# Padded value products, another loop order and two candidate lists in a local attention kernel with routed experts

## The chip, the cores and the metric

The kernel runs on one core of one Trainium2 chip. The metric is the time of one execution in device microseconds (us); less is better. Engines are named as in the profile: PE is TensorE's products, PEld its weight loads, DVE is VectorE, ACT ScalarE, POOL GpSimd, SP SyncE. An engine name with a q (SPq) is that engine's queue, which issues DMAs.

## What is computed

Attention inside blocks of 64 tokens, and then eight experts with one expert per token and at most `capacity` (80) tokens each. Shapes: q, k and v are 8 x 8 x 576 x 64 in float32; 4608 tokens with 512 features; experts of 512 x 1024 x 512.

```python
scores = scale * np.matmul(q_c, k_c.transpose(0, 1, 2, 4, 3))   # blocks of 64
attn = np.exp(scores - np.max(scores, axis=-1, keepdims=True))
attn = attn / (np.sum(attn, axis=-1, keepdims=True) + 1e-09)
x = np.matmul(attn, v_c)                     # then tokens x 512
logits = x @ w_gate
expert_idx = np.argmax(logits, axis=1)
gate_w = softmax(logits)[np.arange(N), expert_idx]
for e in range(E):
    tok_idx = np.where(expert_idx == e)[0]
    if len(tok_idx) > capacity:              # keep those of the highest gates
        gw = gate_w[tok_idx]
        tok_idx = tok_idx[np.argpartition(-gw, capacity)[:capacity]]
    h = np.maximum(x[tok_idx] @ w1[e], 0.0)
    out[tok_idx] = gate_w[tok_idx, None] * (h @ w2[e])
```

Tokens that no expert keeps stay zero in the output.

## The kernel before

Attention. The tokens go through in 18 blocks of 256 tokens, `j`; iteration `i` of the loop takes up several blocks at different stages. `scores(i)` multiplies q and k in tiles of 64 x 64, `maxima(i)` and `shift(i)` on VectorE take the row maximum off, `probs(j)` turns the result on TensorE (`turned`, into the PSUM tile `tp`) and ScalarE writes exp of it to `pT`. `values(j, c)` multiplies `pT` by v for half c of the block: per call 16 products of 64 rows, 64 columns of output and 65 columns of v (the 65th is ones, so that the row sum comes along), each of them two instructions in float32, into the PSUM tile `o`, of which there is one. `divide(j, c)` on VectorE divides by the row sum and `store(j, c)` writes x to HBM. `xtrans(j)` turns x on TensorE, through `tp` as well, and ScalarE copies it. After two blocks `gate_mm` and `gate_sum` (lines 408 to 425) give the logits of four tiles of 128 tokens.

Every engine takes its instructions in the order in which they are written. Small gating steps wait in two queues, `gates` and `bounds_q`, and `fill` (VectorE), `pe_slot` (TensorE) and `act_slot` (ScalarE) put some of them into the written order of the loop.

Routing. A token's key is its gate weight. `lev` compares the keys of four tiles with 256 levels per expert (signs on ScalarE, steps on VectorE) and `tally` counts on TensorE how many lie above each, and `threshold` finds the level above which an expert has at least its capacity; this waits for all 36 tiles, the last eight of them in the interleaved order `LAST`. The keys above it get a place in the list (a mask, a scan and three products, lines 855 to 873), `hot` writes one-hot matrices and 36 products gather one list of at most 128 candidates per expert, `cand`. `rank` compares each candidate with all 128 on VectorE, `select` makes one-hot columns, and `place` puts them into 6 groups of 128 slots (four groups of 32 slots each; an expert has 96). `gi0` and `gi1` are the token rows that are to be gathered, `si` (line 949) those to which the results are written.

Experts. For each group r of 128 slots: gather x rows by an indirect DMA, turn them, layer one, turn, layer two, scatter. The 32-slot quarters of a group belong to experts `groups[r]`: 0001, 1122, 2333, 4445, 5566, 6777. The weights of a layer (2 MB) come whole. Those of experts 0 and 1 are issued early, as eight pieces of 1 MB at the end of iteration 15 (`early_weights`, lines 669 to 677 and 785). Layer one of expert 2 is issued before the experts, layer one of expert 3 after `si` is known, and all the others by `ahead(r)` behind it on SyncE's queue in the order that it lists. `clear(n)` writes zeros to a ninth of the output: four before the experts, five within `ahead(1)`.

## Time and profile before

| what | value |
|---|---|
| median of 3 runs | 290.91 us (290.15 to 293.84) |
| the profiled execution: its time, its span | 290.53 us, 288.7 us |
| busy: PE, PEld, DVE, ACT, POOL | 228.4, 141.9, 118.3, 72.9, 31.0 us |
| instructions: PE and PEld, all | 4193 and 4193, 9408 |
| granted TensorE clock, mean | 0.858 |
| DMA | 85.0 MB, mean 294 GB/s; 418 GB/s from 240 to 260 us |
| instruction fetches (queue q8) | 35 packets, 0.57 MB |
| DMAs issued by SyncE | v 36 x 260 KB, q and k 35 x 512 KB, x 36 x 256 KB, weights 8 x 1024 KB and 12 x 2048 KB, zeros 9 x 1024 KB |

The span runs from the first to the last instruction; the execution's time has a little around it. A busy share is an average over stages with different limits, so the stages are read one by one: the loop, its end, the routing, the experts.

### The profile page before, as it was taken

To read this page: it belongs to the slowest core of one execution; us is meant where nothing else is said; L and a number is where in the kernel's file an instruction comes from. 1 tells how busy PE (TensorE), PEld (TensorE's weight loads), DVE (VectorE), ACT (ScalarE), POOL (GpSimd) and SP (SyncE) were. 2 spreads that over 40 slices of the span, in tenths; PEclk is the share of its full clock that TensorE was granted. 3 is DMA by queue.
4 is the path that set the end of the run, shared out by engine and by line. 5 is a ranking of instruction groups with operands and counts; after the bars stand their busy time and mean duration, and the time that the engine had idled before them with its cause. 6 is when DMAs were issued, how large, how long until landed. Compare 5 with 4: busy or idle time off the path is not lost.

```text
span 288.7 us, 9408 instructions
## 1 busy us (share of the span) xinstructions
PE 228.4 (79%) x4193; PEld 141.9 (49%) x4193; DVE 118.3 (41%) x333; ACT 72.9 (25%) x120; POOL 31.0 (11%) x81
## 2 busy tenths in 40 slices
PE   8466976897787799720644797989999999999990
PEld 6456764776476788620443475833333242423320
DVE  0746587378385578730363056621111111111110
ACT  1212433145444253630154232013001020201000
POOL 2200000002001001000120044260000011100011
PEclk9957799689597779985595559899999999999997
DMA  7999899969889869999749900179999999996011
GB/s 273 338 407 401 280 344 345 333 221 359 279 294 319 270 206 293 396 419 398 293 170 401 346 40 2 35 236 390 413 419 417 419 418 420 419 416 277 1 36 33
DMA packets 28624, 85.00 MB, mean 294 GB/s; under 512 B 3169, under 2 KB 3425, under 8 KB 28577
## 3 DMA queue, kind: packets, MB, share of 16 engines
q1 hardware_dynamic: 27328, 80.86, 74.7%
q0 software_dynamic: 960, 2.88, 2.9%
q8 instruction: 35, 0.57, 0.9%
q10 hardware_dynamic: 288, 0.59, 0.5%
q14 instruction: 13, 0.10, 0.1%
HBM read 64.14 MB, written 20.45 MB: 293 GB/s over the span
## 4 chain that ended last, share of the span: by engine, by line
PE 66%; DMA 10%; issue 9%; ACT 5%; DVE 5%; POOL 2%; POOLq 0%; ACTq 0%; SPq 0%; DVEq 0%
PE hc L193 15%; PE yc L226 14%; PE o L379 9%; PE s L337 7%; DMA v<-in_vv 6%; PE px L359 5%; PE pt L359 4%; PE lg L423 4%; ACT pT L367 4%; PE L L412 3%; DMA qk<-in_qk 2%; DMA ct<-in_cst 2%; PE hpc L211 2%; ACT lv L506 1%; PE pwarm L661 1%
## 5 line engine op out<-in xcount | busy, mean ns | idle before, releaser
L379 PE MATMUL o<-v,pT 64*64 64x65 f32 x1152 | 30.8, 250 | 23.8 <-DMA v<-in_vv 14.3
L193 PE MATMUL hc<-w,xtc 128*32 128x512 f32 x384 | 43.4, 594 | 0.2 <-ACT xtc L183 0.2
L226 PE MATMUL yc<-w,htc 128*32 128x512 f32 x384 | 42.3, 592 | 0.0
L379 PEld LDWEIGHTS o<-v,pT 64*64 64x64 f32 x1152 | 25.7, 159 | 27.1 <-DMA v<-in_vv 14.4
L367 ACT ACTIVATE pT<-pt 128x1024 f32<-128x1024 f32 x18 | 18.4, 1024 | 70.4 <-PE pt L359 70.4
L337 PE MATMUL s<-qk 64*64 64x64 f32 x1152 | 25.9, 249 | 5.9 <-DVE sm L349 2.7
L345 DVE TENSOR_REDUCE mx<-s 128x16 f32<-128x1024 f32 x18 | 22.0, 1222 | 14.1 <-PE s L337 14.0
L337 PEld LDWEIGHTS s<-qk 64*64 64x64 f32 x1152 | 24.0, 164 | 6.8 <-issue 6.5
L226 PEld LDWEIGHTS yc<-w,htc 128*32 128x32 f32 x384 | 12.4, 110 | 28.3 <-issue 28.3
L392 DVE TENSOR_TENSOR x<-o,rc 128x512 f32<-128x512 f32 x36 | 24.9, 691 | 0.8
L193 PEld LDWEIGHTS hc<-w,xtc 128*32 128x32 f32 x384 | 11.8, 110 | 26.0 <-issue 25.5
L405 ACT COPY xT<-px 128x1024 f32<-128x1024 f32 x18 | 18.2, 1012 | 20.6 <-PE px L359 20.5
L388 DVE TENSOR_SCALAR rc<-o 128x8 f32<-128x8 f32 x36 | 5.9, 163 | 42.6 <-PE o L379 42.6
L349 DVE TENSOR_TENSOR sm<-s,mx 128x1024 f32<-128x1024 f32 x18 | 21.8, 1213 | 0.1
L359 PE MATMUL px<-ct,x 64*128 64x64 f32 x288 | 16.3, 266 | 6.9 <-ACT pT L367 6.3
L359 PEld LDWEIGHTS px<-ct,x 64*128 64x128 f32 x288 | 13.2, 171 | 15.0 <-ACT pT L367 14.1
L198 ACT ACTIVATE hsc<-hc 128x512 f32<-128x512 f32 x6 | 3.6, 599 | 63.3 <-PE hc L193 57.9
L231 DVE TENSOR_SCALAR ysc<-yc,gatec 128x512 f32<-128x512 f32 x6 | 4.5, 752 | 33.4 <-PE yc L226 33.4
L359 PE MATMUL pt<-ct,sm 64*128 64x64 f32 x288 | 14.3, 244 | 1.1 <-issue 1.1
L232 POOL DMA_INDIRECT out<-ysc,si x6 | 6.0, 994 | 83.7 <-DMA out<-zero 41.1
L423 PEld LDWEIGHTS lg<-fold,lt 128*128 128x128 f32 x72 | 13.2, 279 | 2.8 <-ACT lt L417 2.4
L423 PE MATMUL lg<-fold,lt 128*128 128x8 f32 x72 | 13.9, 325 | 0.7 <-ACT lt L417 0.7
(135 smaller groups left out, 217.3 us busy)
## 6 DMA issues: line engine op xcount, KB each, us to landing
w<-in_w SPq DMA_DIRECT2D x12, 2048.0 KB, 22.1
qk<-in_qk SPq DMA_DIRECT2D x35, 512.0 KB, 5.9
v<-in_vv SPq DMA_DIRECT2D x36, 260.0 KB, 5.5
xs<-x SPq DMA_DIRECT2D x36, 256.0 KB, 4.1
out<-zero SPq DMA_DIRECT2D x9, 1024.0 KB, 18.0
w<-in_w SPq DMA_DIRECT2D x8, 1024.0 KB, 12.7
qk<-in_qk ACTq DMA_DIRECT2D x1, 512.0 KB, 5.0
ct<-in_cst SPq DMA_DIRECT2D x1, 326.0 KB, 7.4
```

What stands on the lines that cost most here:

```text
L193: nc.tensor.matmul(h[o:o + 32, :], lhsT=xT[r][:, b, o:o + 32], rhs=getw(groups[r][g])[0][:, b, 512 * f:512 * f + 512], start=(b == 0), sto ...
L226: nc.tensor.matmul(y[o:o + 32, :], lhsT=hT[r][c // 4][:, c % 4, o:o + 32], rhs=getw(groups[r][g])[1][:, c, :], start=(c == 0), stop=(c == ...
L337: nc.tensor.matmul(ps[64 * u:64 * u + 64, h, o:o + 64], lhsT=q[64 * h:64 * h + 64, pr, u, :], rhs=k[64 * h:64 * h + 64, pr, u, :], start=T ...
L345: nc.vector.tensor_reduce(mx, PR[j]['s'], axis=AX.X, op=ALU.max)
L349: nc.vector.tensor_tensor(sm.rearrange("p a h k -> p h a k"), PR[j]['s'], PR[j]['mx'][:, :, :, None].to_broadcast([P, 2, 8, 64]), op=ALU.s ...
L359: nc.tensor.transpose(pm[:, u, 64 * a:64 * a + 64], src(a)[rows], ident[rows, rows])
L367: nc.scalar.activation(pT, pm, AF.Exp, scale=0.125)
L379: nc.tensor.matmul(po[64 * u:64 * u + 64, h, 65 * pr:65 * pr + 65], lhsT=PR[j]['pT'][rows, u, a:a + 64], rhs=v[rows, pr, u, :], start=True ...
L392: nc.vector.tensor_tensor(PR[j]['x'][:, c, :].rearrange("p (m h e) -> p h m e", h=2, m=4), po[..., 0:64], rc[:, :, :, None].to_broadcast([ ...
L405: nc.scalar.copy(XT[T][:, j % 2].rearrange("p a u t -> p u a t"), pm.rearrange("p u (a t) -> p u a t", a=8))
L412: nc.tensor.matmul(pl[32 * pr:32 * pr + 32].rearrange("p (r t) -> p r t", r=4), lhsT=wgp[:, pr], rhs=xT[:, pr], start=True, stop=True, til ...
L423: nc.tensor.matmul(lg[:, 4 * n + r, :], lhsT=S['lt', T][:, r], rhs=fold, start=True, stop=True)
```

## The change

- v is laid into four standing tiles `vz` of 128 partitions x 2 x 520, zeroed once. The rows of one head go to the even partitions and to the first half of the columns, those of the other head to the odd partitions and the second half; the rest stays zero. `shift` writes its result with the two heads interleaved to match. A product then has 128 rows and 130 columns and does both heads: 8 products per call of `values` instead of 16. Each v load becomes two, one per head.
- The loop's order: before, `xtrans(i-3)`, `values(i-2, 0)`, `scores(i)`, `maxima`, `values(i-2, 1)`, `shift(i)`, `probs(i-1)`; now `scores(i)`, `maxima`, `xtrans`, `values(., 0)`, `shift`, `probs`, `values(., 1)`. The gate sums and level counts are spread over more iterations (`SUMS`).
- The eight early weight pieces are issued two per iteration from i = 15, the last two behind the stores of block 17. Two clears instead of four stand before the experts, seven within `ahead(1)`.
- The threshold comes from the first 32 tiles (28 to 31 counted on VectorE). Their candidates make a first list, those of tiles 32 to 35 above the same threshold a second one, of at most 128 each. Every rank is a comparison with both lists (256 columns, a constant in `lev_t` settling ties), once for each list, and every placing adds two products. The slots are placed in three parts: group 0, group 1, groups 2 to 5, each with its `targets`.

The core of the diff; `positions(r0, r1)` is the old mask, scan and three products for tiles r0 to r1, `gather_up` the old gathering loop, `listed` the key sum and copy.

```diff
+LATE = 32
...
-                IN['v', j, c] = wk.tile([P, 520], F32, name=f"v{j}_{c}", tag=f"v{c}", bufs=2)
-                nc.sync.dma_start(IN['v', j, c], vv[j, c])
+                for h in range(2):
+                    nc.sync.dma_start(vz[j % 2, c][h:P:2, h], vv[j, c, h])
...
-            sm = PR[j]['sm'] = wk.tile([P, 8, 2, 64], F32, name=f"sm{j}", tag="sm")
+            sm = PR[j]['sm'] = wk.tile([P, 8, 64, 2], F32, name=f"sm{j}", tag="sm")
             nc.vector.tensor_tensor(
-                sm.rearrange("p a h k -> p h a k"), PR[j]['s'],
+                sm.rearrange("p a k h -> p h a k"), PR[j]['s'],
...
-            v = IN['v', j, c].rearrange("p (a u x) -> p a u x", a=4, u=2)
+            v = vz[j % 2, c].rearrange("p h (a u x) -> p h a u x", a=4, u=2)
             for pr in range(4):
-                for h in range(2):
-                    for u in range(2):
-                        rows = slice(64 * h, 64 * h + 64)
-                        a = 64 * (4 * c + pr)
-                        nc.tensor.matmul(
-                            po[64 * u:64 * u + 64, h, 65 * pr:65 * pr + 65],
-                            lhsT=PR[j]['pT'][rows, u, a:a + 64],
-                            rhs=v[rows, pr, u, :], start=True, stop=True)
-            PR[j]['o', c] = po[:, :, 0:260].rearrange("p h (m x) -> p h m x", m=4)
+                o, a = 130 * (pr % 2), 64 * (4 * c + pr)
+                for u in range(2):
+                    nc.tensor.matmul(
+                        po[64 * u:64 * u + 64, pr // 2, o:o + 130].rearrange(
+                            "p (h x) -> p h x", h=2),
+                        lhsT=PR[j]['pT'][:, u, a:a + 64],
+                        rhs=v[:, :, pr, u, :], start=True, stop=True)
+            PR[j]['o', c] = po[:, :, 0:260].rearrange("p j (m x) -> p j m x", m=4)
...
-            nc.vector.scalar_tensor_tensor(ge, U[32]['ph'], 0.5, left, op0=ALU.mult, op1=ALU.is_ge)
+            nc.vector.scalar_tensor_tensor(ge, U[LATE - 4]['ph'], 0.5, left, op0=ALU.mult, op1=ALU.is_ge)
...
+            io_h = gk.tile([P, P, HOT], BF16, name="io_h", tag="io_h", bufs=1)
...
+            vz = {}
+            for b in range(2):
+                for c in range(2):
+                    vz[b, c] = wk.tile([P, 2, 520], F32, name=f"vz{b}{c}", tag=f"vz{b}{c}", bufs=1)
+                    nc.vector.memset(vz[b, c], 0.0)
...
+                p.tensor_copy(io_h, ct[:, C_IO + P:C_IO + 2 * P, None].to_broadcast([P, P, HOT]))
...
-            SUMS = {7: (0, 1), 9: (2,), 13: (3, 4), 15: (5,), 17: (6,)}
+            SUMS = {7: (0, 1), 9: (2,), 11: (3,), 13: (4,), 15: (5,), 17: (6,)}
             for i in range(NP_):
                 now[0] = i
                 if i == 2:
                     late_constants()
+                scores(i)
+                load_qk(i + 3, 0)
+                maxima(i)
+                fill(2)
                 if i >= 3:
                     xtrans(i - 3)
+                pe_slot()
                 if i >= 2:
                     values(i - 2, 0)
                     load_v(i, 0)
                     divide(i - 2, 0)
                     store(i - 2, 0)
-                scores(i)
-                load_qk(i + 3, 0)
-                pe_slot()
-                maxima(i)
-                fill(2)
+                    fill()
+                shift(i)
+                load_qk(i + 3, 1)
                 now[0] = i + 0.5
                 act_slot(2)
+                if i >= 1:
+                    probs(i - 1)
+                    if i == 1:
+                        warm_up(8)
+                fill(2)
                 if i >= 2:
                     values(i - 2, 1)
                     load_v(i, 1)
                     divide(i - 2, 1)
                     store(i - 2, 1)
                     fill()
-                load_qk(i + 3, 1)
-                shift(i)
-                fill(2)
-                if i >= 1:
-                    probs(i - 1)
-                    if i == 1:
-                        warm_up(8)
                 if i >= 4 and i % 2 == 0:
                     gate_mm((i - 4) // 2)
                 if i in SUMS:
...
-                    if i == 13:
-                        gates.append(("v", lambda: lev(12, 20, "av")))
-                    if i == 15:
-                        gates.append(("v", lambda: lev(20, 24, "a")))
-                    if i == 17:
-                        gates.append(("v", lambda: lev(24, 28, "v")))
+                    if i in (11, 13, 15, 17):
+                        gates.append(("v", lambda r=2 * i - 10: lev(r, r + 4, "a")))
                 pe_slot()
                 act_slot(3)
                 fill(2)
-                if i == 15:
-                    for n in range(8):
-                        early_weights(n)
+                if i >= 15:
+                    for n in range(2):
+                        early_weights(2 * (i - 15) + n)
...
+            tail = deque()
+            gate(28, 4, gate_sum((7,)), tail)
+            flush(tail)
+            values(17, 0)
+            xtrans(16)
+            values(17, 1, "s")
+            divide(17, 0, 0)
+            store(17, 0)
+            levels(tail, LATE - 4, 4)
+            flush(tail)
+            for rt in range(LATE - 4, LATE):
+                steps_(nc.vector, rt)
+            tally(LATE - 4, 4)
+            divide(17, 1, 0)
+            store(17, 1)
+            for n in (6, 7):
+                early_weights(n)
+            for n in range(2):
+                clear(n)
             xtrans(17)
             threshold()
...
+            two = ps1.tile([P, 2, 512], F32, name="two", tag="o")
+            S['warm'] = two[:, 1:2, :]
+            incs = [positions(0, LATE)]
+            gate_mm(8)
+            for rt, way, n in ((0, "v", 8), (27, "p", 1), (8, "v", 8), (28, "p", 1),
+                               (16, "v", 8), (29, "p", 1), (24, "v", 3), (30, "a", 1),
+                               (31, "a", 1)):
+                for j in range(n if way != "v" else 1):
+                    hot(rt + j, way, n)
+            late = gate_sum((8,))
+            cands = [two[:, 0, 0:5 * NE].rearrange("p (c e) -> p c e", c=5)]
+            gather_up(cands[0], [*range(0, 27), 30, 31, 27, 28, 29])
+            gate(32, 4, late, tail)
+            flush(tail)
+            keep_warm(6)
+            incs.append(positions(LATE, RT))
+            lists = [listed(cands[0], "a")]
+            def spread(n):
+                for e in range(NE):
+                    nc.tensor.transpose(kr[e][:, P * n:P * n + P],
+                                        lists[n][0][:, e:e + 1].to_broadcast([P, P]), ident)
+            spread(0)
+            hot(LATE, "v", 4)
+            cands.append(ps2.tile([P, 5, NE], F32, name="candb", tag="g"))
+            gather_up(cands[1], range(LATE, RT))
+            lists.append(listed(cands[1], "b"))
+            keep_warm(2)
+            spread(1)
+            rk = gk.tile([P, 2, NE], F32, name="rk", tag="rk", bufs=1)
...
+                for n in range(2):
+                    bt = gk.tile([P, 2 * P], BF16, name=f"bt{e}_{n}", tag="bt")
+                    t0 = C_TAU + P * (1 - n)
+                    nc.vector.scalar_tensor_tensor(
+                        bt, kr[e], lists[n][0][:, e:e + 1], lev_t[:, t0:t0 + 2 * P],
+                        op0=ALU.subtract, op1=ALU.is_gt, accum_out=rk[:, n, e:e + 1])
...
+            tt = target_tiles(mp, "c")
+            gate_w, _, sv = tt
+            gis = []
+            for r0, r1, es in ((0, 1, (0, 1)), (1, 2, (2,)), (2, NR, range(3, NE))):
+                for e in es:
+                    rank(e)
+                    select(e)
+                pl, gi = place(mp, ps2, "g", pairs, "c", r0, r1)
+                gis += [gi[:, r:r + 1] for r in range(r1 - r0)]
+                keep_warm(18 if r0 == 0 else 6)
+                targets(tt, pl, r0, r1)
...
-                    for n in range(4, NT):
+                    for n in range(2, NT):
```

## Rows read from the trace of the kernel before

**Rows 1.** The waits of the whole run: us in total, times, longest.
```profile
PE o L379 <- DMA v<-in_vv: 14.3, 1, 14.3
...
PE o L379 <- issue: 7.3, 4, 2.9
...
PE px L359 <- ACT pT L367: 6.3, 11, 1.2
```
**Rows 2.** Timeline of SyncE's queue: start, duration, what, count.
```profile
112.86 9.33 SPq L676 DMA_DIRECT2D w<-in_w  x8
...
190.26 7.71 SPq L967 DMA_DIRECT2D w<-in_w  x5
```
**Rows 3.** Stretches: length, busy PE, PEld, DVE, ACT, POOL, clock, DMA, GB/s.
```profile
50.00:60.00 10.00, 8.03 (x158) 7.75 (x161) 3.79 (x11) 2.20 (x3) 0.00 (x0) 0.66 0.75 271
170.00:180.00 10.00, 7.57 (x79) 5.64 (x77) 5.82 (x14) 3.36 (x9) 4.76 (x10) 0.84 0.00 0
240.00:260.00 20.00, 20.00 (x188) 6.78 (x184) 2.88 (x4) 1.77 (x3) 2.56 (x3) 1.00 1.02 418
264.00:266.00 2.00, 2.00 (x24) 0.65 (x20) 0.00 (x0) 0.00 (x0) 0.00 (x0) 1.00 0.36 141
```
**Rows 4.** The chain that ended last, one loop iteration: start, us, what.
```profile
35.70 0.63 PE o L379 x32
...
38.32 0.66 PE pt L359 x16
...
39.06 1.03 ACT pT L367
...
40.14 0.71 PE px L359 x16
```
**Rows 5.** The page's costliest groups: busy, mean ns; idle before, its releaser.
```profile
L392 DVE TENSOR_TENSOR x<-o,rc 128x512 f32<-128x512 f32 x36 | 24.9, 691 | 0.8
...
L349 DVE TENSOR_TENSOR sm<-s,mx 128x1024 f32<-128x1024 f32 x18 | 21.8, 1213 | 0.1
```
**Rows 6.** Timeline of PE around 50 us; the last bracket is idle time before.
```profile
46.12 0.46 PE L359 MATMUL px<-ct,x 64*128 64x64 f32 x8 [0.35 <-issue]
...
48.50 0.57 PE L379 MATMUL o<-v,pT 64*64 64x65 f32 x23 [0.37 <-PE s L337]
51.97 0.35 PE L379 MATMUL o<-v,pT 64*64 64x65 f32 x9 [2.89 <-issue]
```
**Rows 7.** The chain that ended last, in the expert stage.
```profile
201.90 3.57 PE hc L193 x32
...
251.46 6.87 PE yc L226 x64
```
**Rows 8.** Timeline of PE: one gate sum at full clock.
```profile
111.85 1.06 PE L423 MATMUL lg<-fold,lt 128*128 128x8 f32 x8
```
**Rows 9.** Timeline from the end of the loop to the slot list.
```profile
139.18 1.13 PE L379 MATMUL o<-v,pT 64*64 64x65 f32 x30 [14.29 <-DMA v<-in_vv]
...
154.29 1.71 ACT L506 ACTIVATE lv<-io_b,bo 128x256 bf16<-128x256 bf16 x4 [1.50 <-DVE bo L501]
...
158.24 1.85 PE L423 MATMUL lg<-fold,lt 128*128 128x8 f32 x8
...
173.41 0.17 DVE L633 TENSOR_TENSOR thr<-thr,low 128x8 f32<-128x8 f32 x1
...
181.26 0.18 DVE L893 TENSOR_REDUCE kc<-two 128x8 f32<-128x24 f32 x1 [2.51 <-PE two L884]
...
184.38 0.34 DVE L901 SCALAR_TENSOR_TENSOR bt<-kr,kc,ct 128x128 bf16<-128x128 f32 x1
...
184.75 1.28 POOL L168 DMA_INDIRECT xgc<-xs,gic  x1 [5.04 <-DVE bt L901]
184.80 0.35 DVE L901 SCALAR_TENSOR_TENSOR bt<-kr,kc,ct 128x128 bf16<-128x128 f32 x1
...
189.09 0.23 DVE L949 TENSOR_SCALAR si<-svc,fl 128x6 int32<-128x6 f32 x1
```

More of the change, by code (lines that the diff above doesn't have):

```diff
@@ L132, in compact, with place @@
         return cand, cb
-    def place(pool, pp, pt, sel, cb, tag, r0=0, r1=NR):
+    def place(pool, pp, pt, pairs, tag, r0=0, r1=NR):
         pl = pp.tile([P, r1 - r0, 5], F32, name=f"pl{tag}{r0}", tag=pt)
@@ new lines, in gather_up, with listed @@
+            def gather_up(cand, order, warm=0):
+                for rt in order:
+                    nc.tensor.matmul(
+                        cand.rearrange("p c e -> p (c e)"), lhsT=S[rt],
+                        rhs=comp[:, rt].rearrange("p c e -> p (c e)"),
+                        start=rt == order[0], stop=rt == order[-1])
+            def listed(cand, nm):
+                kc = gk.tile([P, NE], F32, name=f"kc{nm}", tag=f"kc{nm}", bufs=1)
+                nc.vector.tensor_reduce(
+                    kc, cand[:, 2:5, :].rearrange("p c e -> p e c"), axis=AX.X, op=ALU.add)
+                cb = gk.tile([P, 5, NE], BF16, name=f"cb{nm}", tag=f"cb{nm}", bufs=1)
+                nc.scalar.copy(cb, cand)
+                return kc, cb
@@ new lines, in select, with pairs @@
+            def select(e):
+                for n in range(2):
+                    sel[e, n] = gk.tile([P, SL], BF16, name=f"sel{e}_{n}", tag=f"sel{e}_{n}", bufs=1)
+                    nc.vector.tensor_scalar(sel[e, n], io_b[:, 0:SL], rk[:, n, e:e + 1], 1.0,
+                                            op0=ALU.subtract, op1=ALU.is_equal)
+            def pairs(e, j):
+                return [(sel[e, n][:, 32 * j:32 * j + 32], lists[n][1][:, :, e]) for n in range(2)]
+            keep_warm(8)
@@ L980, in attention_moe @@
             part(3, 0, si[:, 0:1])
-            experts(ep, pp, lambda r: gi1[:, r - 1:r] if r else gi0, si, gate, weights.get, "c",
+            experts(ep, pp, lambda r: gis[r], si, gate_w, weights.get, "c",
                     ahead)
```

220 lines of the change are left out of this document (65 added, 155 removed).

## The prediction

> **What bounds the kernel now.** I read the waits first, then the chain that ended last, then the timelines of the stretches it names. The longest single wait is not arithmetic: TensorE stands 14.3 us for one v tile [rows 1]. The DMA queue shows why. At the end of iteration 15 SyncE puts eight weight pieces of 1 MB on the queue in one go, which takes it 9.33 us [rows 2], and the v tiles 16 and 17 are issued behind them. So the profile has four stages with four limits: the attention loop, to 124.9; the stop for v16, to 139.18 (14.3 after it); the routing tail, from there to the slot list `si` at 189.09 [rows 9]; and the experts, from `si` to the end of the span at 288.7, 99.6 us.
>
> In the loop the DMA queues are well used but not the limit of a clean iteration. From 35.70 to the next such point at 40.85 the chain is scores, two products with v, the turn of the probabilities, its exp on ScalarE, the turn of x: 5.15 us, of which the exp (1.03) holds TensorE still because the turn that follows wants its PSUM bank [rows 4]. Where gating products stand there instead, the wait is covered: over the whole run it is 6.3 us in 11 places [rows 1]. The loop loses more to stops in the middle of a homogeneous group: 23 of the 32 instructions of one product ran, then nothing for 2.89 us, then 9 more, and no semaphore is named [rows 6]; four such stops inside the products make 7.3 us [rows 1]. About 255 loads and products lie between that stop and the short one at 46.12. I read it as TensorE's instruction stream running dry. The granted clock falls with it: 0.66 in the ten microseconds around it [rows 3].
>
> In the expert stage TensorE never waits for weights, but the slack is small. The weight stream starts at 190.26 [rows 2], 1.2 us after `si`, and the queues fall idle inside 264 to 266, at about 264.7 by the busy share of 0.36 [rows 3]. Three 2.1 MB layers follow the second layer of expert 5; at 418 GB/s they take 5.0 us each, so that one landed near 249.7, and it is first needed at 251.46 [rows 7]: 1.8 us of slack. Between 170 and 180 the queues moved nothing [rows 3].
>
> **Part by part, against the profiled 288.7 us.** *The stop for v16.* The pieces now go out two per iteration from i=15, each pair after that iteration's v, and the last two behind the stores of block 17. Ahead of v16 stand 2 MB (5.0 us) and ahead of v17 two such pairs, with no q or k left to load and an iteration or more to land. I take the stop as gone: -14.3. The bytes go into the loop's last iterations and into the idle stretch of the tail. What could be late next is one iteration's DMA: v, stores and pieces make 3.15 MB or 7.5 us, near an iteration's own length, which the early issue of v covers. The 36 more v loads (72 of 130 KB for 36 of 260) cost SyncE issue time, at most the 1.17 us that one of the eight pieces took on a full queue [rows 2]; TensorE's iteration hides them, and if it didn't, two more issues an iteration would be 2.3 us late. Zeroing the four padded tiles (1040 columns, 1.2 us each at the rate of rows 5) lies in the time in which the first q and k land: taken as 0, at most +2, since the constants are queued on SyncE behind v loads that wait for it.
>
> *The padded products.* Each call has 16 instructions of 130 columns on two column tiles, for 32 of 65 columns on four. The nearest row for full-height column tiles is the expert product: 32 instructions of 512 columns on four tiles in 3.57 us [rows 7], that is 111 ns each, 446 ns per tile, 0.87 ns a column. Then 130 columns take 113 ns, two tiles give 57 ns, and 16 make 0.91 us, for 0.63 now [rows 4]. By the same columns the old call would be 0.45, so 0.18 of it is ends or issue; the new call lies between 0.91 and 1.09, +0.35 taken. Over the 28 calls of iterations 4 to 17: +9.8. The ends: if only the number of instructions counted, 16 of 20 ns (-0.3 a call, -8); if each weight load stood alone with its product, see the last rival.
>
> One rule weighs here. The row just used shows loads of one column tile hidden under products of another at the same rows: 3.57 us is the columns alone. The Trainium skill ("TensorE: Matmul & The Clock Gate", section Part 3, The mechanism) says that a weight load overlaps a running product only when the row groups differ, and the padding makes all row groups the same; by it the sum would be that last rival's. The trace speaks against it for 32-column tiles; no row shows it for 64.
>
> *The new order.* Scores, turn of x, first product, turn of the probabilities, second product: the turns no longer follow each other, so the exp's 6.3 us go. In their place comes a wait that the old order had not: the second product needs the PSUM bank that `divide(i-2, 0)` reads. From the end of the first product that is 0.15 to notice, and 1.1 for the division (of which 0.69 the multiplication [rows 5]), while TensorE has only the turn of 0.66 [rows 4] to do: 0.6 an iteration, x14 = +8.3. `shift` (1.21 [rows 5]) comes behind that division and next to it stand the scores; with gating products in between they are not held. Bounds: 0 if tallies fill the gap, 14 if the gating operations that `fill` puts into the division lengthen it.
>
> *Instruction stops.* A fifth fewer instructions per iteration, and an iteration no shorter, give a block of 255 about 5.5 us to run instead of 4.1. Most stops are shorter than that difference; I take 6 of the 7.3 away, and 4 us (an estimate: three or four stretches like the one at clock 0.66, about 1.2 each) of slow products after them: -10. Bounds 0 and -14. Loop in all: 9.8 - 6.3 + 8.3 - 10 = +1.8.
>
> *The tail to the threshold.* Now, from 139.18 to the gate sum of tiles 28 to 31 at 158.24, three rounds of four signs on ScalarE (1.71 each [rows 9]) and one on VectorE are still to be counted; the new schedule counts up to tile 23 in the loop. Left (estimates: 0.17 to 0.23 for each dependent small step of VectorE, as in rows 9, and the durations above) are the product (0.95), turn, gating product and second product (2.8), division (1.1), rest of the gate (0.8), level bounds (0.7), four signs (1.7), counting (0.6): 8.7 for 19.1, -10.4. Then 158.24 to the threshold at 173.41 [rows 9] ran two gates in a row, one behind the last turn, copy, gating product and sum. The threshold now waits for tiles 28 to 31 alone: gate sum 1.85 [rows 9], gate 2.0 (nine steps of 0.22), division 1.1, bounds 0.7, four counts 0.9, division 1.1, turn 0.75, threshold 0.7: 9.1 for 15.2, -6.1.
>
> *The two lists.* From the threshold to the candidates' key sum was 7.85 (173.41 to 181.26 [rows 9]). The first list has the same length, and under it lie the last tiles' sums; their gate, ranks of position, one-hots and second list stand behind it: 10.0, +2.2. From there to the first gather 3.5 (to 184.75 [rows 9]); now four rankings of 256 columns for two of 128, +0.7. From the first gather to `si` 4.3: five experts at 0.42 (184.38 to 184.80 [rows 9]) and 2.2 of placing and flags. Each expert now has two rankings and two selections; 128 more columns cost 0.15 at the 1.21 us per 1024 of rows 5, so 2 x 0.57, x 6 experts = 6.8, and 4.2 for two more placings and the targets between: 11.0, +6.7. Tail in all: -10.4 - 6.1 + 2.2 + 0.7 + 6.7 = -6.9.
>
> *The experts.* The weights from layer one of expert 3 on wait for `si`, which is now 11 us behind the first gather instead of 4.3, so the stream and no longer TensorE ends this stage. Two more clears (2.1 MB, 5.0 us) are in it: 5.0 - 1.8 of slack - 1.0 for gathers that ran before it + 0.2 and more for products that restart after a wait: 99.6 becomes 102.0, +2.4.
>
> *Sum.* 288.7 + 1.8 - 14.3 - 6.9 + 2.4 = 271.7. The profiled run took 290.53, 1.8 more than its span and 0.4 under the median of 290.91; with the same 1.8, 273.5.
>
> **The rivals.** *The loop gains as well:* tallies fill the new waits and no stop is left. For it: the gaps have the length of a tally. Against: the division is on VectorE, which the loop keeps busy too. 273.5 - 8.3 - 3 = 262. *The tail gains nothing:* the split of the lists costs what the earlier threshold saves, since everything there is one chain of short steps on VectorE. 273.5 + 6.9 = 280. *The stop only moves:* the eight pieces reach the queue in a loop whose DMA share is already high, and v17 or the stores behind them come as late as before, so the change doesn't do what it is laid out for. 273.5 + 14.3 = 288. *Slower:* the weight loads of the full-height products are not hidden. Full-height loads of 128 columns with short products run 8 in 1.06 us [rows 8], so 66 ns for 64 columns; 66 + 113 = 179 ns each and 16 make 2.9 us a call, 1.9 above my value, x32 calls = +61: 334. It decides once a call takes 1.75 us: 0.75 x 32 = 24 lifts 273.5 past 2% above the median.
>
> **How the numbers follow.** Chances: forecast 0.52, loop gains 0.17, tail gains nothing 0.14, stop moves 0.12, loads not hidden 0.05. Two per cent of the median, which is what a measurement of this kernel can tell from no change, lie at 285.1 and 296.7. Faster: 0.52 + 0.17 + 0.14 = 0.83; within 0.12; slower 0.05. The range goes from 259 (below the loop rival by the uncertainty of its stops) to 288 (the stop that moves); outside are the last rival and the edges.
>
> **What would show it.** Right: no wait of TensorE for v above 2 us; a product call of 0.9 to 1.1 us at full clock; the second product waiting for the first division; `si` about 11 us behind the first gather; the weight stream without a gap from `si` on and TensorE waiting for it once, about 7 to 8 us, near layer one of expert 6. Wrong: calls above 1.5 us, a v wait after iteration 15, a loop longer than 130 us, or expert products that never wait.

## The result, and the profile after

The changed kernel took 279.73 us (median of 4 runs, 277.05 to 284.64) beside 290.53 before: a ratio of 0.955, 95% interval 0.948 to 0.962. Measured a second time (after_again) it took 277.41 beside 291.70: 0.951, 0.943 to 0.959. The profiled execution took 277.05 us with a span of 275.3. Some executions of a kernel are 1 to 3% longer than others of it (one of old_order_levels_v 12%); the ratios below leave them out, the medians don't, and the profiles of old_products (292.22 us), one_list (276.32) and warm_slots (270.67) are of such executions.

TensorE's waits from 8 to 120.4, the end of the loop (us in total, times, longest), for [rows 1]:

```profile
PE o L374 <- PE pt L356: 8.8, 16, 1.0
PE s L334 <- issue: 5.7, 5, 2.7
PE pt L356 <- issue: 0.3, 1, 0.3
```

The wait for v is gone, and so is the one for the exp. All but 0.7 of the stops without a releaser lie in the first 24 us. New are sixteen waits of the second product. The releaser named, `pt`, is not the one: in the timeline of one iteration

```profile
61.97 0.71 PE L356 MATMUL pt<-ct,sm 64*128 64x64 f32 x16
...
62.40 0.68 DVE L388 TENSOR_TENSOR x<-o,rc 128x512 f32<-128x512 f32 x1
...
63.18 1.11 PE L374 MATMUL o<-vz,pT 128*64 128x130 f32 x16 [0.50 <-PE pt L356]
```

the turn ends at 62.68 and the division, which reads the bank, at 63.08; the product starts 0.1 later. A call of `values` takes 1.11 us at full clock. The stretch 20 to 120 as a whole (length; PE, PEld, DVE, ACT, POOL; clock, DMA share, GB/s), before and after:

```profile
20.00:120.00 100.00, 81.49 (x2443) 68.59 (x2445) 67.41 (x163) 39.65 (x56) 5.75 (x23) 0.84 0.89 308
```

```profile
20.00:120.00 100.00, 89.40 (x2134) 72.65 (x2136) 75.85 (x191) 45.11 (x67) 8.08 (x35) 0.98 0.95 326
```

The timeline from the loop's end to the slot list, for [rows 9]:

```profile
119.77 0.71 PE L356 MATMUL px<-ct,x 64*128 64x64 f32 x16
120.41 1.11 PE L374 MATMUL o<-vz,pT 128*64 128x130 f32 x16
...
123.98 1.69 ACT L499 ACTIVATE lv<-io_b,bo 128x256 bf16<-128x256 bf16 x4
126.91 1.70 ACT L499 ACTIVATE lv<-io_b,bo 128x256 bf16<-128x256 bf16 x4 [1.24 <-DVE bo L494]
129.85 1.70 ACT L499 ACTIVATE lv<-io_b,bo 128x256 bf16<-128x256 bf16 x4 [1.24 <-DVE bo L494]
132.80 1.70 ACT L499 ACTIVATE lv<-io_b,bo 128x256 bf16<-128x256 bf16 x4 [1.24 <-DVE bo L494]
134.72 1.85 PE L419 MATMUL lg<-fold,lt 128*128 128x8 f32 x8
...
143.07 0.17 DVE L622 TENSOR_TENSOR thr<-thr,low 128x8 f32<-128x8 f32 x1
...
155.26 0.18 DVE L855 TENSOR_REDUCE kcb<-candb 128x8 f32<-128x24 f32 x1 [1.90 <-PE candb L848]
...
159.71 1.27 POOL L165 DMA_INDIRECT xgc<-xs,gic  x1 [6.82 <-DVE svc L155]
...
170.93 0.23 DVE L945 TENSOR_SCALAR si<-svc,fl 128x6 int32<-128x6 f32 x1
```

Four rounds of four signs, 2.94 us apart, still stand between the loop and the logits of tiles 28 to 31. The experts, from the timeline and from TensorE's waits behind 170:

```profile
170.49 5.32 PE L190 MATMUL hc<-w,xtc 128*32 128x512 f32 x32
```

```profile
PE yc L223 <- DMA w<-in_w: 1.4, 1, 1.4
PE hc L190 <- DMA w<-in_w: 0.3, 1, 0.3
```

The first call of layer one runs at half clock (3.57 at full [rows 7]), and the weights are waited for. The term by term comparison of the two profiled executions:

| stage | before | predicted | after |
|---|---|---|---|
| start to the first product of block 16, without the wait | 124.9 | 126.7 | 120.4 |
| wait for v16 | 14.3 | 0 | 0 |
| to the logits of tiles 28 to 31 | 19.1 | 8.7 | 14.3 |
| to the threshold | 15.2 | 9.1 | 8.35 |
| to the key sum of the last list | 7.85 | 10.0 | 12.2 |
| to the first gather | 3.5 | 4.2 | 4.45 |
| to `si` | 4.3 | 11.0 | 11.2 |
| to the end of the span | 99.6 | 102.0 | 104.4 |

Loop -4.5, stop -14.3, tail (the five rows from the logits to `si`) +0.6, experts +4.8: -13.4, from 288.7 to 275.3.

### The profile page after: what moved, and what is told of

It is laid out like the page before. It is cut to its first block, busy times and chain, and to the rows that moved or that the text cites. A ratio compares the mean times of both kernels' runs of the same rounds, so it can differ in the third digit from the quotient of the medians.

```text
span 275.3 us, 8364 instructions
## 1 busy us (share of the span) xinstructions
PE 235.8 (86%) x3613; PEld 142.2 (52%) x3613; DVE 130.7 (47%) x374; ACT 74.1 (27%) x125; POOL 33.2 (12%) x93
## 4 chain that ended last, share of the span: by engine, by line
PE 68%; DMA 9%; DVE 7%; ACT 7%; issue 6%; POOL 0%; POOLq 0%; ACTq 0%
PE yc L223 13%; PE hc L190 12%; PE o L374 10%; DMA w<-in_w 9%; PE s L334 8%; PE pt L356 5%; ACT xT L401 4%; PE px L356 4%; PE lg L419 4%; PE L L408 4%; PE pw L689 2%; DVE bt L903 2%; ACT lv L499 2%; PE two L650 2%; PE hpc L208 1%
## 5 line engine op out<-in xcount | busy, mean ns | idle before, releaser
L374 PE MATMUL o<-vz,pT 128*64 128x130 f32 x576 | 41.5, 284 | 8.9 <-PE pt L356 8.8
L190 PE MATMUL hc<-w,xtc 128*32 128x512 f32 x384 | 46.9, 613 | 0.4 <-DMA w<-in_w 0.3
L374 PEld LDWEIGHTS o<-vz,pT 128*64 128x64 f32 x576 | 32.7, 139 | 12.8 <-PE pt L356 10.6
L334 PE MATMUL s<-qk 64*64 64x64 f32 x1152 | 23.6, 232 | 5.7 <-issue 5.7
L334 PEld LDWEIGHTS s<-qk 64*64 64x64 f32 x1152 | 20.7, 144 | 13.5 <-issue 6.9
L197 DVE TENSOR_SCALAR hsc<-hc 128x512 f32<-128x512 f32 x6 | 4.2, 692 | 25.1 <-PE hc L190 25.1
L212 DVE COPY htc<-hpc 128x512 f32<-128x512 f32 x6 | 4.2, 692 | 21.7 <-PE hpc L208 21.7
L356 PE MATMUL pt<-ct,sm 64*128 64x64 f32 x288 | 13.4, 234 | 1.1 <-issue 0.3
L356 PE MATMUL px<-ct,x 64*128 64x64 f32 x288 | 13.8, 239 | 0.4 <-DVE x L388 0.4
L356 PEld LDWEIGHTS pt<-ct,sm 64*128 64x128 f32 x288 | 10.8, 143 | 5.1 <-ACT xT L401 3.7
L499 ACT ACTIVATE lv<-io_b,bo 128x256 bf16<-128x256 bf16 x28 | 12.1, 498 | 3.7 <-DVE bo L494 3.7
```

Source lines behind the costliest of these rows:

```text
L190: nc.tensor.matmul(h[o:o + 32, :], lhsT=xT[r][:, b, o:o + 32], rhs=getw(groups[r][g])[0][:, b, 512 * f:512 * f + 512], start=(b == 0), sto ...
L334: nc.tensor.matmul(ps[64 * u:64 * u + 64, h, o:o + 64], lhsT=q[64 * h:64 * h + 64, pr, u, :], rhs=k[64 * h:64 * h + 64, pr, u, :], start=T ...
L356: nc.tensor.transpose(pm[:, u, 64 * a:64 * a + 64], src(a)[rows], ident[rows, rows])
L374: nc.tensor.matmul(po[64 * u:64 * u + 64, pr // 2, o:o + 130].rearrange("p (h x) -> p h x", h=2), lhsT=PR[j]['pT'][:, u, a:a + 64], rhs=v[ ...
L499: nc.scalar.activation(lv, io_b, AF.Sign, bias=bo[:, rt:rt + 1], scale=-1.0)
```

## The experiments

All of them change the kernel after, except where said. The stages of each profiled execution, from the same rows as above; "loop" is the start of the transposes of block 15 (px, 119.77 above), and the logits are those of tiles 28 to 31. Times are medians, stages are those of the one profiled execution:

| kernel | time, ratio to before (95%) | loop | to logits | to threshold | to gather | to `si` | to end |
|---|---|---|---|---|---|---|---|
| before | | 124.17 | 34.07 | 15.17 | 11.34 | 4.34 | 99.6 |
| after | 279.73, 0.955 (0.948 to 0.962) | 119.77 | 14.95 | 8.35 | 16.64 | 11.22 | 104.4 |
| after_again | 277.41, 0.951 (0.943 to 0.959) | 120.36 | 14.93 | 8.35 | 16.63 | 11.22 | 102.0 |
| at_once | 291.07, 1.004 (0.998 to 1.010) | 118.73 | 28.93 | 8.35 | 16.63 | 11.23 | 102.8 |
| old_order | 277.76, 0.962 (0.953 to 0.970) | 113.99 | 19.99 | 8.72 | 15.94 | 11.23 | 102.2 |
| old_products | 289.88, 0.998 (0.994 to 1.003) | 134.41 | 16.53 | 8.43 | 16.02 | 11.23 | 103.8 |
| half_products | 290.70, 1.000 (0.993 to 1.006) | 130.77 | 16.49 | 8.84 | 15.91 | 11.23 | 104.0 |
| levels_v | 277.25, 0.951 (0.943 to 0.958) | 121.69 | 15.43 | 8.84 | 16.06 | 11.23 | 102.2 |
| old_order_levels_v | 275.41, 0.940 (0.931 to 0.949) | 115.74 | 16.52 | 8.83 | 16.14 | 11.23 | 102.3 |
| early_clears | 274.15, 0.932 (0.923 to 0.940) | 121.22 | 14.94 | 8.84 | 15.92 | 11.22 | 100.3 |
| one_list | 274.37, 0.931 (0.922 to 0.940) | 123.73 | 16.28 | 8.85 | 14.77 | 8.31 | 102.5 |
| combined | 270.06, 0.927 (0.920 to 0.933) | 114.12 | 16.27 | 8.35 | 16.63 | 11.22 | 99.2 |
| warm_slots | 269.81, 0.919 (0.911 to 0.928) | 116.06 | 18.48 | 8.83 | 15.92 | 11.03 | 98.5 |
| warm_both | 271.55, 0.928 (0.920 to 0.935) | 118.20 | 17.98 | 8.31 | 15.80 | 11.02 | 98.5 |

**at_once** gives the pieces back their place:

```diff
-                if i >= 15:
-                    for n in range(2):
-                        early_weights(2 * (i - 15) + n)
+                if i == 15:
+                    for n in range(8):
+                        early_weights(n)
```

> All eight early weight pieces go on the queue together at the end of iteration 15, as before the change; the rest is the changed kernel (277 us, no wait for v). If spreading the pieces removed the stop: TensorE waits 12 to 15 us for v of block 16 again, and the time rises by 11 to 15 us, to 288 to 292. Rival, that the tail behind it has slack in which the stop is absorbed (pieces, zeros and the first expert layer are then on chip earlier): the wait is there, but the time rises by 6 us at most.

Measured 291.07, the time of before. The timeline of its first products of block 16:

```profile
131.63 2.00 PE L374 MATMUL o<-vz,pT 128*64 128x130 f32 x16 [12.19 <-DMA vz<-in_vv]
136.17 1.11 PE L374 MATMUL o<-vz,pT 128*64 128x130 f32 x16
```

The wait is back with 12.19 us, and the product behind it runs at half clock; in all the logits stand 14.0 us later, counted from the loop. Spreading eight DMA issues is worth as much as the whole net gain.

**old_order** moves the calls of the loop back into the old order and leaves everything else.

```diff
-                scores(i)
-                load_qk(i + 3, 0)
-                maxima(i)
...
                 if i >= 2:
                     values(i - 2, 0)
...
-                shift(i)
...
+                scores(i)
+                load_qk(i + 3, 0)
+                pe_slot()
+                maxima(i)
...
-                    probs(i - 1)
...
                     values(i - 2, 1)
...
+                shift(i)
...
+                    probs(i - 1)
```

> The changed kernel with the loop order of before; the padded products stay. The changed kernel's loop ends (first product of block 16) at 120.4 us, that of before at 124.9. If fewer TensorE instructions made the loop shorter, by fewer stops in the instruction stream: it ends within 3 us of 120.4 and the stops stay below 2 us in all up to there. If the order did it: it ends 5 to 9 us later, with the wait for the exp back (6 us in all) and no more stops than in the changed kernel.

**old_products** keeps the order and goes back to 64-row products of 65 columns and to the old v tiles; **half_products** keeps the padded tiles and cuts each product in two.

```diff
-                        po[64 * u:64 * u + 64, pr // 2, o:o + 130].rearrange(
-                            "p (h x) -> p h x", h=2),
+                        po[64 * u:64 * u + 64, pr // 2, o + 65 * h:o + 65 * h + 65],
...
-                        rhs=v[:, :, pr, u, :], start=True, stop=True)
+                        rhs=v[:, h, pr, u, :], start=True, stop=True)
```

> The changed kernel with the 64-row products of before (and v loaded whole); the new order stays. A call is 0.63 instead of 1.05 us, which by the chain of scores, first product, division and shift is worth 0.4 to 0.8 us an iteration, 6 to 11 us in all. If instruction stops decide: they are back (6 us or more up to the end of the loop, with stretches of lower clock), and the loop ends between 117 and 126, not earlier. If the order decides: it ends between 110 and 115.

> Each padded product is made in two of 65 columns: the same columns, rows and zeros, twice the instructions for the values. If the number of instructions decides: stops of 1 to 3 us return, 4 us or more of them up to the end of the loop, which ends 4 to 10 us later (124 to 130). Rival, that the full-height products keep the clock up and so made the loop shorter: it ends within 2 us of 120.4, apart from the weight loads that the second half adds, and the granted clock stays above 0.95 in the loop.

The same stretch, 20 to 120, in half_products, in old_products and in old_order:

```profile
20.00:120.00 100.00, 86.03 (x2436) 73.90 (x2432) 70.15 (x170) 42.32 (x61) 6.58 (x28) 0.96 0.88 298
```

```profile
20.00:120.00 100.00, 79.52 (x2346) 66.08 (x2341) 65.95 (x161) 39.16 (x57) 5.45 (x23) 0.85 0.86 290
```

```profile
20.00:120.00 100.00, 89.53 (x2149) 72.05 (x2145) 74.53 (x191) 45.19 (x65) 7.64 (x33) 1.00 0.98 344
```

Same order, same number of instructions, other height (old_products to half_products): no gain and no loss, 289.88 and 290.70, while the clock goes from 0.85 to 0.96. The end of the loop in old_products, 134.41, is outside both ranges that were expected of it (110 to 126), and its time, without the stop for v16, is still that of before. Same height, same columns in all, half the instructions (half_products to after): 11 to 13 us by the medians (290.70 to 279.73 and 277.41), and in the profiled executions 11 of 11.9 lie in the loop (130.77 to 119.77). A call of half_products is hardly longer, as its timeline shows,

```profile
70.57 1.15 PE L375 MATMUL o<-vz,pT 128*64 128x65 f32 x32 [0.55 <-PE pt L356]
```

so the price is not in the products but between them. Its stops without a releaser (us in total, times, longest)

```profile
PE o L375 <- issue: 4.3, 5, 1.7
...
PE pt L356 <- issue: 1.7, 1, 1.7
PE ph L517 <- issue: 0.9, 1, 0.9
```

are 6.9 us up to 131, all behind 24, where after has 0.7. The clock (0.96 for 0.98) leaves about 2 more in 100 us, and an iteration without a stop is some 0.1 longer (6.25 for 6.15 between two transposes of x), 1.5 in all: by this estimate nearly 10 of the 11. half_products did nearly what was expected if the number of instructions decides; the clock stayed above 0.95, as the rival had it, but the loop didn't stay short. Over the same stretch, from 24 to the end of the loop, such stops make 11.2 us in before, 11.2 in old_products and 2.8 in old_order: 7 to 11 us in the three kernels with some 4190 TensorE products, 0.5 to 4.0 in the eleven with some 3600. That the stops are instruction fetches is argued from the counts alone: 35 fetch packets in the three kernels with the larger number of products, 30 or 31 in the others; no run counts them one by one.

The order does not help. In old_order the loop ends 5.8 us earlier than in after, and the time is the same: 277.76 beside 279.73 and 277.41. Neither expectation had this (within 3 us, or 5 to 9 us later). One pair of profiles is little, since the loop's end moves: in the five kernels here with padded products in the old order it lies between 114.0 and 118.2, in the six in the new order between 118.7 and 123.7, 5.3 us apart on average. In old_order the wait for the exp is back, and a short one behind the scores (up to 115):

```profile
PE px L356 <- ACT pT L364: 5.2, 12, 1.2
...
PE o L374 <- PE s L334: 2.6, 13, 0.3
```

Together they are 1.0 less than the 8.8 that the new order waits for the division; where the rest of the difference comes from is not shown. All four combinations of order and products were measured. With the old products the loop ends at 124.2 in the old order (before, whose count schedule differs too) and at 134.4 in the new one (old_products), with the padded ones at 114.0 and 119.8. So by these profiles the new order costs 6 to 10 us in the loop, and the padded products gain 10 to 15. Why the time did not follow the loop in old_order is the next experiment's subject.

**levels_v** and **old_order_levels_v** count tiles 12 to 27 on VectorE, in the order after and in the old one.

```diff
-                        gates.append(("v", lambda r=2 * i - 10: lev(r, r + 4, "a")))
+                        gates.append(("v", lambda r=2 * i - 10: lev(r, r + 4, "v")))
```

> The four rounds of counts for tiles 12 to 27 go from ScalarE to VectorE, nothing else. Theory (the serial rounds behind the loop set when the logits of tiles 28 to 31 start, so they ate what the shorter loop gave): a round, 2.94 us in the changed kernel with four signs of 0.42 us in it, falls to about 2.0 (four counts of 0.22 us on VectorE, as in its last round), the logits of 28 to 31 start at about 131 in place of 134.7, and the time falls by 3.5 to 4.5 us, to about 276. Rival A (the slots and the weight stream set that point, not the rounds): the logits stay at 134 to 135 and the time at 279.7. Rival B (VectorE, busy 70 to 85% in the loop, becomes its bound when it gets the counts): the loop ends later than 119.8 and the time is 280 or more.

> The padded products with the loop order of before, and the counts of tiles 12 to 27 on VectorE. With the old order the transposes of pair 15 stood at 114.0, 5.8 us earlier than in the changed kernel, but five rounds of signs were still to come then and the logits of 28 to 31 stood at 134.0, 0.7 earlier. Theory (the rounds are what holds that point): five rounds at about 2.0 in place of 2.94 bring the logits to about 129 and the time to about 273, some 5 us under the 277.8 of the old order with signs. Rival (with the old order something else holds that point, as the stores or the weight stream): the logits stay at 133 to 134 and the time at 277 to 278.

In old_order five rounds of signs are left when the loop ends, from 120.28, and the logits come 19.99 us behind the loop. With four of the five on VectorE (old_order_levels_v) they come after 16.52, 3.5 less for four rounds; the rounds are 2.02 us apart for 2.94:

```profile
125.12 0.87 DVE L504 TENSOR_SCALAR lv<-io_b,bo 128x256 bf16<-128x256 bf16 x4
...
127.13 0.88 DVE L504 TENSOR_SCALAR lv<-io_b,bo 128x256 bf16<-128x256 bf16 x4
...
132.26 1.85 PE L419 MATMUL lg<-fold,lt 128*128 128x8 f32 x8
```

So the rounds hold that point, and the loop's earlier end had been spent waiting for them; the time falls from 0.962 of before to 0.940, and the intervals don't meet. levels_v missed: 15.43 for 14.95, and 277.25. In VectorE's timeline

```profile
128.39 0.17 DVE L384 TENSOR_SCALAR rc<-o 128x8 f32<-128x8 f32 x1 [2.38 <-PE o L374]
...
128.57 0.28 DVE L504 TENSOR_SCALAR lv<-io_b,bo 128x256 bf16<-128x256 bf16 x1
...
130.37 0.47 DVE L504 TENSOR_SCALAR lv<-io_b,bo 128x256 bf16<-128x256 bf16 x2
...
132.00 0.88 DVE L504 TENSOR_SCALAR lv<-io_b,bo 128x256 bf16<-128x256 bf16 x4
134.02 0.88 DVE L504 TENSOR_SCALAR lv<-io_b,bo 128x256 bf16<-128x256 bf16 x4
```

the later rounds are 2.02 us apart here too, but what four of them gain (3.7) is lost ahead of them. The first count starts 6.9 us behind the loop instead of 4.2. Of this 2.1 is block 16 at half clock in this execution (5.55 us from the transposes to its second product, for 3.46 in after); the rest is VectorE's written order, which puts the division of that product ahead of the counts, where ScalarE's signs could start beside it. And the first round takes 3.4 us, since its four counts stand between that division and the gating steps. In one_list and half_products, which count with signs and also ran block 16 at half clock, the logits come after 16.28 and 16.49; beside those the counts gained 0.9 and 1.1. Neither rival had that.

**early_clears** and **one_list** try the two halves of the end.

```diff
             now[0] = NP_
+            for n in range(2, 5):
+                clear(n)
             xtrans(15)
...
-            for n in range(2):
+            for n in (0, 1, 5, 6):
                 clear(n)
             xtrans(17)
...
-                    for n in range(2, NT):
+                    for n in range(7, NT):
```

> Five of the seven 1 MB clears of the output that the queue issues behind the first gathers are issued earlier, in the two stretches in which the queue had little to do (about 126 to 142 and 150 to 170). Theory (the experts were 4.8 us longer than before because the transfers, full from 171 to 251, ended last): TensorE's waits for weights in the last third (0.27 and 1.40 us, and the stretched calls around them, 3.7 us in all) go, the experts fall from 104.4 to about 100.5 and the time to about 276. What is left over the 99.6 of before is the first call at half clock (5.32 us in place of 3.57), which this run doesn't touch. Rival A: the clears stand in front of the stores of x and of the weights, si comes later than 170.9 by 2 us or more and the time stays at 279 to 283. Rival B: TensorE itself is the bound there, experts unchanged at 104.

```diff
-                for n in range(2):
-                    bt = gk.tile([P, 2 * P], BF16, name=f"bt{e}_{n}", tag="bt")
-                    t0 = C_TAU + P * (1 - n)
+                for n in range(1):
+                    bt = gk.tile([P, P], BF16, name=f"bt{e}_{n}", tag="bt")
+                    t0 = C_TAU + P
```

> Only the first candidate list is ranked, selected and placed; the candidates of tiles 32 to 35 are left out of the slots (their list is still built). A row of ranks is 128 columns in place of 256, one row and one selection per expert in place of two. Theory (placing is on the path: si sets the start of the experts): from the first gather to si 11.2 us falls to 5 to 7, si to 165 or 166, and the time by 4 to 6 us, to about 274 to 276. Rival (the experts end with the stream of transfers, and that is held by the queue and not by si): si comes as early, but the end stays within 2 us of 279.7.

early_clears came out as expected: experts 100.3, and TensorE waits for no weights any more. Two stretches in which the queues stood mostly idle in after, and the same in early_clears:

```profile
130.00:140.00 10.00, 6.98 (x67) 5.91 (x69) 3.81 (x19) 3.90 (x10) 1.56 (x7) 0.51 0.29 113
160.00:170.00 10.00, 6.21 (x70) 4.42 (x68) 8.43 (x50) 0.00 (x0) 3.17 (x4) 0.86 0.27 86
```

```profile
130.00:140.00 10.00, 5.92 (x55) 4.87 (x57) 3.11 (x19) 3.70 (x10) 0.45 (x3) 0.51 1.02 416
160.00:170.00 10.00, 6.13 (x71) 4.30 (x72) 8.71 (x53) 0.00 (x0) 2.56 (x3) 0.89 0.93 372
```

In one_list the first gather to `si` takes 8.31 for 11.22, a smaller gain than expected; ahead of the gather it gains another 1.4 from the logits on (23.62 for 24.99). The experts take 102.5, no longer than in after, so the earlier `si` comes back whole: the time falls by 3 to 5, about as expected.

**after_again, combined, warm_slots, warm_both.** combined puts the edits of old_order, levels_v and early_clears together; the other two add products that nobody reads: warm_slots the first two lines here, in `place` for groups 2 to 5, warm_both the others as well, in `sum_levels`.

```diff
+            if warm is not None and g % 3 == 2:
+                warm(4)
...
+                if now[0] > NP_:
+                    w = ps2.tile([P, 2 * P], F32, name=f"pw{T}", tag="g")
+                    for _ in range(4):
+                        nc.tensor.matmul(w, lhsT=ones_b, rhs=io_b, start=True, stop=True)
```

> The changed kernel as it is, on the chip and beside the kernels of this call, since these differ from it by 1 to 3%. Both theories: 277 to 281. Theory (the loop's end shifts from execution to execution with the clock, by 118.7 to 123.7 in the profiled executions of four kernels with the same loop): stages counted from the transposes of pair 15 repeat, 15 us to the logits of 28 to 31, 51 to si, 104 from si to the end. Rival: they move too.

> The padded products and the placing of the changed kernel, with the loop order of before, the counts of tiles 12 to 27 on VectorE and five of the clears issued early: the three edits of old_order, levels_v and early_clears in one. Theory (each works in a stage of its own): from the transposes of pair 15 to the logits of 28 to 31 16.5 us as in old_order_levels_v, si at about 168, the experts 100.3 as in early_clears in place of 102.3: a span of 268 to 270 and a time of 271 to 273, some 6 to 8 under the changed kernel. Rival (the clears, issued while a shorter tail leaves less room, hold up the stores of x and the gathers): si later than 171 and 275 or more.

> As combined, and four idle products behind each of the last five experts' placing products, where TensorE waits 0.74 us for each selection; nothing waits for them. Theory (the first call of the experts runs at half clock, 5.32 us in place of 3.57, because TensorE was mostly idle in the six microseconds ahead of it): the granted clock there stands at 1.00, the first call takes 3.6 to 4 us, and the time is 1.5 to 2 us under combined. Rival (the experts end with the stream of transfers): the call is shorter, the end is not, and the time is within 0.5 us of combined.

> As warm_slots, and four idle products behind the sums of each round of counts after the loop, where TensorE waits 1.14 us for each round. Theory (the stretch from the logits of 28 to 31 to the threshold runs at half clock, with products of 2.00 us in place of 1.11, transposes of 1.11 in place of 0.71 and logits of 1.85 in place of 1.06): the clock stays at 1.00 there, the 8.8 us from these logits to the threshold become 6 to 7, the second list is 1 us earlier too, and the time is 2 to 4 us under warm_slots. Rival (these stretches wait for VectorE's chain, not for TensorE): within 1 us of warm_slots; or the idle products delay the sums, and it is slower.

after_again repeats each stage behind the loop to 0.02 us up to `si`; the experts differ, 102.0 for 104.4, and TensorE waits 0.5 us for weights there instead of 1.7. combined beats both kernels: 270.06 us, 0.927 of before and 2.5 to 3.5% under the change. Its gain adds up by stages: 6 us in the loop and 3 to 5 in the experts, less 1.3 to the logits. Alone, the old order and the counts on VectorE gained nothing that the medians show. In warm_slots the clock from 160 to 170 is 1.00 (0.67 in combined, of which 0.50 up to 166). The first call of the experts takes 3.64 us, but in combined it took only 3.86 already,

```profile
166.15 3.86 PE L190 MATMUL hc<-w,xtc 128*32 128x512 f32 x32
```

```profile
169.62 3.64 PE L192 MATMUL hc<-w,xtc 128*32 128x512 f32 x32 [0.30 <-ACT xtc L182]
```

where the other kernels since the change have 4.4 to 5.4; why combined has less is open. The times, 269.81 and 270.06, are not told apart, and the intervals of the ratios overlap: the expected 1.5 to 2 us are neither shown nor excluded. warm_both is a miss: it is not faster than warm_slots, 271.55 for 269.81, and the stage from the logits to the threshold takes 8.31, as in combined (8.35). Its logits come 17.98 us behind the loop for 16.27 in combined, but only part of this is the price of the idle products. The rounds are 2.01 us apart, as without them. A stop within the transposes of block 15 makes 0.6; warm_slots has such a stop too, and its logits come after 18.48 without those idle products. What the idle products cost is seen in front of the logits, which come 1.9 us behind the last counts, for 1.1 in combined. They don't keep the clock either:

```profile
135.37 1.01 PE L618 MATMUL pw<-io_b,ones_b 128*128 128x256 bf16 x4
136.18 1.71 PE L421 MATMUL lg<-fold,lt 128*128 128x8 f32 x8
```

four of them take 0.60 us at first and 1.01 by now.

## Why the prediction came out as it did

The time was 273.5 by the forecast and 277 to 280 by measurement, inside the range. That it is so near is luck in part, because the terms missed on either side: the tail by +7.5, the loop by -6.3, the experts by 0 to +2.4.

*The stop for v16, -14.3:* right, and shown by at_once.

*The step that failed is "To the logits of 28 to 31", 8.7 for 19.1.* It stood on the sentence that the new schedule counts up to tile 23 in the loop. In the trace the first signs come at 100.53,

```profile
100.53 1.31 ACT L499 ACTIVATE lv<-io_b,bo 128x256 bf16<-128x256 bf16 x3
```

and the loop ends with tiles 0 to 11 counted; four rounds were left, not one. Announcing the sums earlier (`SUMS`) fills a list that is worked off one step at a time, each round behind the bounds and the total of the one before. I should have read from before how much of the list the loop works off (eight tiles, from 117.29 on), not what the loop puts on it. I also misread what is left in before: beside the three rounds of signs stand two on VectorE and not one, five rounds in all.

```profile
117.29 0.51 ACT L506 ACTIVATE lv<-io_b,bo 128x256 bf16<-128x256 bf16 x1 [2.30 <-DVE bo L501]
...
150.99 0.87 DVE L511 TENSOR_SCALAR lv<-io_b,bo 128x256 bf16<-128x256 bf16 x4
...
157.15 0.87 DVE L511 TENSOR_SCALAR lv<-io_b,bo 128x256 bf16<-128x256 bf16 x4
```

14.3 instead of 8.7 is this. The three more rounds are 8.8 us, more than the 5.6 between the two, since the second product and its division, which the sum put ahead of the rounds, run beside them. old_order_levels_v shows the rounds to be the holder.

*Lists, +2.2:* measured +4.3. By the timeline 1.7 of the missing 2.1 is that the gate of tiles 32 to 35 ran with gating products of 1.94 and sums of 1.88 us, for 1.07 and 1.06 in the loop; no run tests it alone. *To the threshold, first gather, `si`:* 8.35, 4.45 and 11.2 for 9.1, 4.2 and 11.0; right.

*The loop, +1.8:* measured -4.5, with terms of mixed fate. A call cost 1.11 us at full clock, just above the 0.91 to 1.09 of the bounds, the wait for the division 8.8 for 8.3, and the exp's wait is gone: right. *Instruction stops, -10:* the stops behind 24 us fell from 11.2 to 0.7, where I took 6 of 7.3 away, and the clock rose from 0.84 to 0.98; the count of instructions alone is worth 11, shown by half_products. My reason for them, that a block of 255 takes 4.1 us, is an average: the block of [rows 6] ran in 2.95, from 46.12 to 49.07. What I put too high is the padding, +9.8: from old_products to half_products, the same instructions at twice the height, the time is the same. There the stops fell from 11.2 to 6.9 and the clock rose, so something paid for the longer calls; which of the two is not shown. And I put the order too low: +2.0 for 5.8 between old_order and after, and 10.2 between before and old_products. Of the two mis-sized terms the products weigh more, -0.2 in the forecast for -10 to -15, so that the loop was 6 better than forecast.

One rule was set against the row of the 32-column tiles: the Trainium skill ("TensorE: Matmul & The Clock Gate", section Part 3, The mechanism) has weight loads overlap products only of other row groups. The calls here speak against it for 64-column tiles too: 16 in 1.11 us, 69 ns each. Load and product one after the other would be 179 by [rows 7, 8], and 89 even if the two column tiles ran side by side (estimates).

*Experts, +2.4:* 102.0, and measured 104.4 and 102.0. The mechanism was half right. The stream does hold this stage, and early_clears takes that out (100.3); but TensorE waits 1.7 us for it, not 7 to 8. Another 1.75 are the first call at half clock, which I had not seen coming. TensorE now idles 0.74 us for each selection ahead of it, and with idle products in those gaps (warm_slots) the clock stands and the call takes 3.64. That this alone explains the 5.32 is not shown, since combined has the same gaps and 3.86.

Two rivals were each right about a stage, that the tail gains nothing (+0.6) and that the loop gains as well. As both happened, neither gives the time for its reason: that the 280 of the first lies beside the median of 279.73 is luck, since its sum has a loop 6.3 us longer than the measured one.

## What to carry to other kernels

When a stop goes, look at what had been running beside it: a serial list of small steps on other engines is then next, and its length, not the schedule that announces it, is to be read from the trace. Fewer, wider instructions can be worth more than the columns that the padding adds, where stops without a releaser and a low granted clock show that TensorE's instruction count is a limit. Test an order by undoing it alone: here several edits came together, and one of them cost about 6 us in the loop that no total shows, because the rounds behind the loop took up whatever time it left; only with shorter rounds behind it does a gain appear (old_order_levels_v, a ratio of 0.940 for 0.962).

## What the runs showed of the hardware

- 32 instructions of 65 columns and 16 of 130, at the same height, take 1.15 and 1.11 us a call; the kernel with the former is 11 to 13 us slower, with 6.9 us of stops that no semaphore explains, for 0.7.
- Doubling the height of the 32 instructions of a call with zeros cost nothing: 289.88 and 290.70 us, at granted clocks of 0.85 and 0.96 from 20 to 120.
- The same loop (the counts apart) ended between 118.7 and 123.7 us in the profiled executions of after, after_again, at_once, levels_v, early_clears and one_list. Behind it, logits to threshold took 8.35 to 8.85 and threshold to first gather 15.9 to 16.6 where the edits left them alone; loop to logits took 14.9, or 16.3 in one_list, where block 16 ran at half clock.
- Four idle products of 256 columns in each round of 2.0 us did not hold the clock (the last ones 0.25 us each, for 0.15 at first); between the placing products they did (1.00 from 160 to 170, for 0.67).
